# Offset columns from the partition number, one transfer for the hash matrix, and a replanned order: hashed attention and a feed-forward layer on one core

## The chip, the core and the metric

The kernel runs on one core of a Trainium2 chip. The metric is the device time of one execution in microseconds (us), lower is better. A core has TensorE (matrix products, PE in the profile; PEld are its weight loads), VectorE (DVE), ScalarE (ACT), GpSimd (POOL) and SyncE (SP, which here only issues transfers). Transfers are issued on a queue of SyncE or of ScalarE and are carried out by 16 DMA engines.

## What is computed

q, k and v have 4 batches of 8 heads, 768 positions and 64 columns; proj has 64 x 6 values. The feed-forward weights are 512 x 2048 and 2048 x 512. Every position of q and of k is hashed to a bucket by the signs of its six products with proj, and a query attends only to keys of its bucket:

```python
q_bits = (np.einsum('bhsd,dk->bhsk', q, proj) > 0).astype(np.int64)
k_bits = (np.einsum('bhsd,dk->bhsk', k, proj) > 0).astype(np.int64)
q_bucket = np.sum(q_bits * powers, axis=-1)
k_bucket = np.sum(k_bits * powers, axis=-1)
mask = q_bucket[:, :, :, None] == k_bucket[:, :, None, :]
scores = np.where(mask, scale * np.matmul(q, k.transpose(0, 1, 3, 2)), -1000000000.0)
attn = softmax(scores)             # with 1e-9 added to the sum
x = np.matmul(attn, v)             # heads side by side: 3072 x 512
out = gelu(x @ w_in) @ w_out
```

## The kernel before

**Staging.** A pass goes over a batch and some of its query positions; batch 0 is split in two passes (the first 256 queries, then 512), the other three are one pass each. Within a pass, a unit is 128 queries of one head: scores against all 768 keys (L987 in plain fp32 for batch 0, L989 and L990 in halves of 16 bits after it), their row maximum on VectorE (L993), exponential on ScalarE (L1007), a transposition, and the product with v. The feed-forward layer takes 256 queries at a time: 24 groups of hidden products (L1396), gelu, and output products (L1478).

**Hashing.** The bits are added to the operands of the score product as extra rows, so that a differing bit costs a large amount. For this each head's q and k are projected (`project`, L936 for batch 0, L695 later) with the matrix `hash32` or `hash16`, which hold proj and its negative side by side; ScalarE takes the sign with a small bias per partition (`sign`, L942, L701), and the signs are written as mask rows into the operands (`mask`, by `affine`, L460 and L464). The bias breaks ties: it is -TINY for some columns and +TINY for the others. It is an input of the program, `offset`, one value for each of 128 partitions.

**Set-up.** ScalarE's queue loads proj twice, into the upper and the lower 64 partitions of `praw` (L383, L384), and `offset` into `offs` (L386). VectorE writes the negative of proj beside it (L406) and copies both to `hash32` (L409). Two columns of bias are wanted, `off` and `off16`, since the two kinds of heads have their columns at different partitions. `set_up` makes them: GpSimd builds shift matrices from the identity (`copies`, L531), VectorE rounds `offs` to 16 bits (`narrow`, L538), TensorE moves it by two products (`spread`, L542), and VectorE copies the result to `both_offs` (`take`, L545). Each sign waits for this copy (`offs_ready`).

**What sets the order.** Nearly all work is a list of steps, each with an engine (or several to choose from), a cost in us, a key and the steps that it needs. `Plan.order` plays them through: whenever an engine is free, it takes the ready step with the lowest key, and some steps get their engine in this way too. `START` says when an engine begins. The keys come from the unit's number t and the numbers in `PAR`; the feed-forward products have keys from 1000 on. The outcome is a fixed order for each engine, in which instructions wait for their operands; a waiting instruction holds all behind it on its engine. SyncE's transfers stand in that order as well. Where TensorE has nothing ready, the plan may put in products of a blank tile (L419, up to 128 steps of four); nobody reads their result.

Of the kernel before, what the change touches and what calls it, by code (L numbers as in the profile page):

```python
# [38 lines left out]
    STICK=-82.49, LP_DVE=168.72, LP_Pool=131.55, KM=22.79, KM_ACT=-0.38, KM_DVE=21.62, KM_Pool=77.76, RN=-228.07,  # L39
    RT=-120.93, RC_ACT=-187.97, RC_DVE=104.4, XH_ACT=-169.94, XH_DVE=-58.71, XH_Pool=153.81, XL_DVE=2.29,  # L40
    XL_Pool=-84.29, VB=75.91, GU_DVE=376.97, GU_Pool=-283.34, SH_DVE=-141.74, SH_ACT=169, SH_Pool=-102.03,
    SF_DVE=106.59, SF_ACT=-91.62, SF_Pool=-105.46, SU=255.56, NM_DVE=139.91, NM_ACT=-81.24, NM_Pool=114.06,
    NM_SP=-82.67, NL_DVE=426.56, NL_Pool=109.97, NK_DVE=140.93, NK_ACT=118.24, NK_Pool=-152.1, Z=-98.92, VS0=-226.8,
    H0=1350.75, HL=-150.29, VS=-186.92, G2=45.62, HQ=-153.69, VQ=-322.44, in0=210.99, out0=-154.22, in1=106.47,
    out1=18.08, in2=-133.65, out2=-122.24, in3=462.36, out3=2.34, H1=390.62, H2=235.99, H3=74.68, H4=-91.19,
    H5=-484.96, H6=160.92, H7=182.63, MEV=-284.82, MGE=-95.53, MSP=-95.01, V0=-96.78, QK0=-173.32, QK1=188.62,
    QK2=101.09, MX0=117.31, MX1=-38.76, MX2=-22.52, EX0=-485.91, EX1=468.22, EX2=-110.13, NR0=17.49, NR1=108.73,
    NR2=80.71, HI0=-258.98, HI1=22.07, HI2=232.15, LO0=35, LO1=-160.32, LO2=2.65, PV0=-16.06, PV1=-698.65,
    PV2=-277.98, TR0=151.7, TR1=219.82, TR2=2.67, V1=-251.7, V2=66.98, Sin0=-94.82, Sin1=-40.21, Sin2=62.47,
    Sin3=-65.73, Sout0=12.07, Sout1=20.19, Sout2=-141.49, Sout3=15.82, Lin=572.06, Pin=97.32, Qin=138.76,  # L50
    Cin=-105.62, Min=-18.36, Lout=375.6, Pout=89.64, Qout=24.03, Cout=365.45, Mout=-620.71, G0=52.67, G1=-55.39,
    G3=17.42, G4=-204.1, G5=26.67, G6=177.05, G7=213.7, DUP0=-160.19, DUP1=-74.32, DUP2=842.69, LOW0=-36.13,
    LOW1=-187.95, LOW2=-265.14, PRJ0=293.66, PRJ1=118.05, PRJ2=248.42, MSK0=-16.31, MSK1=-34, MSK2=-4.17,
    DI_ACT=44.21, DI_DVE=54.03, DI_Pool=-87.05, WS_ACT=-12.67, WS_DVE=-97.95, WS_Pool=-164.14, WH_ACT=60.25,
    WH_DVE=76.08, WH_Pool=10.25, WL_ACT=-103.41, WL_DVE=147.58, WL_Pool=27.65, VH_ACT=90.01, VH_DVE=123.18,
    VH_Pool=-76.83, RND_ACT=-125.63, RND_DVE=144.01, RND_Pool=117.51, HI_ACT=-106.91, HI_DVE=738.91, HI_Pool=34.78,
    EV_ACT=28.16, EV_DVE=4.77, EV_Pool=-35.31, GH_ACT=-33.98, GH_DVE=180.18, GH_Pool=55.02, NS0=123.24, NS1=-168.39,
    NS2=409,
# [22 lines left out]
class Plan:  # L81
# [16 lines left out]
    START = {"PE": 1.1, "DVE": 4.2, "Pool": 1.3, "SP": 0.7, "ACT": 2.7}  # L98
# [176 lines left out]
def tile_bucket_attention_moe(  # L275
# [98 lines left out]
    def buf(step):  # L374
# [22 lines left out]
    offs16 = const.tile([P, 1], BF16, tag="offs16", name="offs16")  # L397
# [116 lines left out]
    def set_up():  # L514
# [22 lines left out]
        def narrow():  # L537
            nc.vector.tensor_copy(out=offs16, in_=offs)  # L538
# [1031 lines left out]
```

## Time and profile before

| | us |
|---|---|
| three timed runs | 884.11, 886.59, 887.58 (median 886.59) |
| span of the profiled execution, first to last instruction | 882.8 |
| TensorE busy | 861.6 |
| VectorE, ScalarE, GpSimd busy | 668.3, 626.8, 404.9 |

The span is that of one profiled execution; the timed runs have no profile, and their median lies 3.8 us above it. Busy time of TensorE counts the blank products too. Granted clock is the share of TensorE's 2.4 GHz that it was given in a stretch: 1.00, or 0.50 for 1.2 GHz. In the rows, "idle before" is the time for which an engine had nothing to run ahead of an instruction, and the name behind the arrow is what ended it.

### The profile page before, as it was taken

How to read it: one execution, taken by the hardware profiler on the slowest of the kernel's cores; microseconds unless marked ns; L12 is line 12 of the kernel's file. 1: busy time of each engine (PE TensorE's matmuls, PEld its weight loads, DVE VectorE, ACT ScalarE, POOL GpSimd, SP SyncE). 2: the span in 40 equal slices, each digit the busy share in tenths (PEclk: the TensorE clock that was granted, in tenths of full speed). 3: DMA queues.
4: the chain of work that ended last, by engine and by line, in shares of the span. 5: the costliest groups of instructions: out<-in, count | busy, mean ns of one | idle time of the engine just before them, and what ended most of it. 6: DMA issues, size and time to landing. Idle time of an engine off the chain costs nothing. (4 is left out here: it accounts for less than half of the span.)

```text
span 882.8 us, 17207 instructions
## 1 busy us (share of the span) xinstructions
PE 861.6 (98%) x6419; PEld 554.4 (63%) x6419; DVE 668.3 (76%) x1360; ACT 626.8 (71%) x1061; POOL 404.9 (46%) x524
## 2 busy tenths in 40 slices
PE   7999988999999999999999999999999999999998
PEld 4666565666747656657656656665666566676663
DVE  5888888898898998998887988889887883212122
ACT  3788767898888887988797977887886773222221
POOL 2367545676667656656373655454553230000000
PEclk6999999999999999999999999999999999999999
DMA  9652475116888697768675969586866593000000
GB/s 326 191 157 70 141 210 140 41 48 134 151 154 168 142 189 156 149 135 175 127 162 110 212 130 186 107 178 129 153 123 117 99 185 55 25 1 25 1 26 24
DMA packets 281955, 111.48 MB, mean 126 GB/s; under 512 B 228624, under 2 KB 269584, under 8 KB 281872
## 3 DMA queue, kind: packets, MB, share of 16 engines
q1 hardware_dynamic: 281568, 110.39, 57.3%
q8 instruction: 50, 0.82, 0.4%
q14 instruction: 33, 0.27, 0.1%
q10 hardware_dynamic: 304, 0.00, 0.0%
HBM read 42.73 MB, written 6.29 MB: 56 GB/s over the span
## 5 line engine op out<-in xcount | busy, mean ns | idle before, releaser
L1396 PE MATMUL hp<-x,Win 128*128 128x256 f16 x2304 | 268.0, 272 | 0.5 <-ACT h L1406 0.2
L1478 PE MATMUL hp<-Wout,g 128*128 128x512 f16 x1152 | 263.3, 379 | 0.0
L1396 PEld LDWEIGHTS <-Win 128*128 128x128 f16 x2304 | 223.7, 98 | 41.6 <-issue 5.4
L993 DVE TENSOR_REDUCE rows<-s 128x1 f32<-128x768 f32 x192 | 180.7, 949 | 17.5 <-PE s L987 8.4
L1478 PEld LDWEIGHTS <-g 128*128 128x128 f16 x1152 | 110.8, 98 | 124.6 <-issue 4.1
L1007 ACT ACTIVATE p<-s,rows 128x768 f32<-128x768 f32 x141 | 139.2, 988 | 19.6 <-POOL rows L464 12.7
L1406 ACT ACTIVATE h<-hp,ffs 128x512 f32<-128x512 f32 x96 | 65.4, 681 | 89.5 <-PE hp L1396 87.9
L989 PE MATMUL s<-Q 88*128 88x384 f16 x304 | 99.4, 327 | 3.9 <-ACT wraw L1007 2.0
L990 PE MATMUL s<-K 128*128 128x384 f16 x304 | 99.2, 326 | 0.0
L464 DVE TENSOR_SCALAR g<-h,ffs 128x512 f16<-128x512 f32 x29 | 15.3, 526 | 96.0 <-ACT h L1434 68.3
L1448 DVE SCALAR_TENSOR_TENSOR g<-h,ffs,g 128x512 f16<-128x512 f32 x96 | 77.8, 822 | 6.6 <-ACT g L460 4.2
L998 POOL TENSOR_SCALAR rows<-rows,hs 128x1 f32<-128x1 f32 x68 | 48.1, 708 | 75.0 <-DVE rows L993 60.9
L486 POOL TENSOR_TENSOR K<-raw,Q 64x768 f16<-64x768 f32 x41 | 73.5, 1793 | 3.4
L1161 PE MATMUL hp<-pt,vhl 128*64 128x512 f16 (+1 forms) x864 | 74.9, 327 | 0.2 <-ACT h L1406 0.2
L1025 DVE SCALAR_TENSOR_TENSOR hl<-p,rows,hl 128x768 f16<-128x768 f32 x60 | 62.7, 1046 | 3.8 <-ACT hl L460 3.8
L1161 PEld LDWEIGHTS <-vhl 128*64 128x64 f16 x864 | 47.8, 110 | 25.4 <-issue 7.3
L1007 ACT ACTIVATE wraw<-s,rows 128x768 f32<-128x768 f32 x51 | 50.3, 985 | 12.0 <-POOL rows L464 7.1
L464 POOL TENSOR_SCALAR Q<-sign 24x384 f16<-24x384 f16 (+1 forms) x59 | 38.4, 651 | 36.6 <-ACT sign L701 13.4
L464 POOL TENSOR_SCALAR rows<-rows 128x1 f32<-128x1 f32 x87 | 31.9, 367 | 45.9 <-ACT p L1007 32.8
L464 POOL TENSOR_SCALAR raw<-raw,hs 64x768 f32<-64x768 f32 x41 | 44.0, 1072 | 5.8 <-ACT Q L460 2.3
L1434 ACT ACTIVATE h<-h 128x2048 f32<-128x2048 f32 x24 | 45.9, 1911 | 0.4
L989 PEld LDWEIGHTS <-Q 88*128 88x128 f16 x304 | 29.7, 98 | 25.0 <-issue 6.9
(169 smaller groups left out, 1302.5 us busy)
## 6 DMA issues: line engine op xcount, KB each, us to landing
raw<-qk SPq DMA_DIRECT2D x26, 384.0 KB, 3.6
vraw<-v SPq DMA_DIRECT2D x24, 384.0 KB, 4.1
wraw<-w_in SPq DMA_DIRECT2D x16, 512.0 KB, 4.5
wraw<-w_out SPq DMA_DIRECT2D x16, 512.0 KB, 4.1
out<-o SPq DMA_DIRECT2D x11, 512.0 KB, 3.5
K<-Q SPq DMA_DIRECT2D x28, 96.0 KB, 2.8
Q<-qk SPq DMA_DIRECT2D x6, 384.0 KB, 8.2
Q<-Q SPq DMA_DIRECT2D x20, 96.0 KB, 2.7
```

The lines of the kernel that those rows point to most:

```text
L464: on.tensor_scalar(out=o, in0=x, scalar1=scale, scalar2=bias, op0=ALU.mult, op1=ALU.add)
L486: on.tensor_tensor(out=o, in0=x, in1=y, op=ALU.subtract)
L989: nc.tensor.matmul(to, aq[kk, qs], ak[kk, n], start=True, stop=False)
L990: nc.tensor.matmul(to, bq[:, qs], bk[:, n], start=False, stop=True)
L993: nc.vector.tensor_reduce(out=nm, in_=both(sp), axis=AX.XY, op=ALU.max, negate=True)
L1007: nc.scalar.activation(out=buf(ex).rearrange("p (b k) -> p b k", b=2), in_=both(sp), func=AF.Exp, scale=sc, bias=nb, accum_out=ssum,)
L1025: nc.vector.scalar_tensor_tensor(out=buf(hi)[:, 1], in0=buf(ex), scalar=r, in1=buf(hi)[:, 0], op0=ALU.mult, op1=ALU.subtract,)
L1161: nc.tensor.matmul(pv[j * D : (j + 1) * D], buf(vh)[:, tv, kt, j * D : (j + 1) * D], pt_all[:, slots(j), tp * KT + kt], start=kt == 0 and ...
L1396: nc.tensor.matmul(buf(pair[0])[:, j * ch[1] : (j + 1) * ch[1]], win_hl[:, f0 // WB1, tw, pr, f0 % WB1 : f0 % WB1 + P], x[:, tx, pr, : ch[1]],
L1406: nc.scalar.activation(out=values_of()[:, 2 * fp : 2 * fp + 2, :nt], in_=buf(pair[0])[:, : 2 * nt].rearrange("p (j k) -> p j k", j=2), fun ...
L1448: nc.vector.scalar_tensor_tensor(out=gt[:, 1, s2, :nt], in0=h[:, s2, :nt], scalar=sg, in1=gt[:, 0, s2, :nt], op0=ALU.mult, op1=ALU.subtract,)
L1478: nc.tensor.matmul(buf(banks[u]).rearrange("p (c f) -> p c f", c=NWB), gt[:, tg, f, u * P : (u + 1) * P], wout_hl[:, :, tw, ft], start=ft ...
```

## The change

- `offset` stays an input but is no longer loaded. A column of partition numbers (`place`) is made by an iota on GpSimd; VectorE masks it to 5 bits, compares it with 6, 12, 18 and 24, and adds the results up to `off` and `off16`: eight VectorE instructions outside the plan. The steps `copies`, the old `narrow`, `spread` and `take` go, and the sign no longer waits for them.
- proj is loaded by one transfer into all 128 partitions, with a source that names it twice.
- The two writes behind it (negative, and the copy to `hash32`) become a step of the plan on VectorE (`narrow`, key -1000); the projections of batch 0 (L936) and the largest value of proj need it.
- Planned costs are nearer to recorded durations, `START` of VectorE is 4.9 instead of 4.2 and of GpSimd 1.6 instead of 1.3, and all numbers in `PAR` are new, so that every engine's order is another one.

```diff
-    nc.scalar.dma_start(out=praw[:D, :NBIT], in_=proj)
-    nc.scalar.dma_start(out=praw[D:, :NBIT], in_=proj)
-    offs = const.tile([P, 1], F32, tag="offs", name="offs")
-    nc.scalar.dma_start(out=offs, in_=offset)
+    nc.scalar.dma_start(out=praw[:, :NBIT], in_=proj.unsqueeze(0).broadcast_to([2, D, NBIT]))
+    place = const.tile([P, 1], I32, tag="place", name="place")
+    nc.gpsimd.iota(place, pattern=[[0, 1]], base=0, channel_multiplier=1)
...
     nc.vector.tensor_scalar(
-        out=praw[:, NBIT:], in0=praw[:, :NBIT], scalar1=-1.0, scalar2=None, op0=ALU.mult
+        out=place, in0=place, scalar1=D // 2 - 1, scalar2=None, op0=ALU.bitwise_and
     )
-    nc.vector.tensor_copy(out=hash32[:, : 2 * NBIT], in_=praw)
+    for n, by in enumerate((2.0, 1.0, 2.0, 1.0)):
+        nc.vector.tensor_scalar(
+            out=over[:, n : n + 1], in0=place, scalar1=float((n + 1) * NBIT), scalar2=by * TINY,
+            op0=ALU.is_ge, op1=ALU.mult,
+        )
+    nc.vector.scalar_tensor_tensor(
+        out=off, in0=over[:, 0:1], scalar=-TINY, in1=over[:, 1:2], op0=ALU.add, op1=ALU.subtract
+    )
+    nc.vector.tensor_tensor(out=over[:, 4:5], in0=over[:, 2:3], in1=over[:, 3:4], op=ALU.subtract)
+    nc.vector.scalar_tensor_tensor(
+        out=off16, in0=off, scalar=over[:, 1:2], in1=over[:, 4:5], op0=ALU.subtract, op1=ALU.add
+    )
...
         def narrow():
-            nc.vector.tensor_copy(out=offs16, in_=offs)
-
-        def spread():
-            for n in range(2):
-                nc.tensor.matmul(buf(sp)[:, n : n + 1], shift[:, n], offs16, start=True, stop=True)
-
-        def take():
-            nc.vector.tensor_copy(out=both_offs, in_=buf(sp)[:, :2])
+            nc.vector.tensor_scalar(
+                out=praw[:, NBIT:], in0=praw[:, :NBIT], scalar1=-1.0, scalar2=None, op0=ALU.mult
+            )
+            nc.vector.tensor_copy(out=hash32[:, : 2 * NBIT], in_=praw)
...
-        c = add("Pool", 0.9, copies, -1000.0, [])
-        z = add("DVE", 0.07, narrow, -1000.0, [])
-        sp = add("PE", 0.2, spread, -1000.0, [c, z], takes="hp")
-        o = add("DVE", 0.07, take, -1000.0, [sp])
-        free(sp, [o])
-        m = add("DVE", 0.1, largest, key, [])
+        z = add("DVE", 0.25, narrow, -1000.0, [])
+        m = add("DVE", 0.1, largest, key, [z])
...
-        pp = add("PE", 0.75, project, key + PAR[f"PRJ{cl}"], [space], takes="hp", table="quarter", act=0.5)
-        sg = add("ACT", 0.1 + 0.833e-3 * HS + 0.186, sign, key + PAR[f"PRJ{cl}"], [pp, offs_ready])
+        pp = add("PE", 0.75, project, key + PAR[f"PRJ{cl}"], [space, hash_ready], takes="hp", table="quarter", act=0.5)
+        sg = add("ACT", 0.1 + 0.833e-3 * HS + 0.186, sign, key + PAR[f"PRJ{cl}"], [pp])
...
-                        "PE", (1.85 if bare else 1.32) * part, lambda j=j, hidden=hidden: hidden(j), LATE + n,
+                        "PE", (1.85 if bare else 1.31) * part, lambda j=j, hidden=hidden: hidden(j), LATE + n,
...
-                step = add("PE", (1.84 if bare else 1.31) * part * len(us) / (nt // P), output, LATE + n + PAR["G2"], needs)
+                step = add("PE", (1.84 if bare else 1.295) * part * len(us) / (nt // P), output, LATE + n + PAR["G2"], needs)
```

The keys that the prediction names are built from these numbers (scores t - QK, row maxima t - MX, remainders t + LO; the last digit is 1 for batch 0's second pass and 2 for the later batches): QK1 188.62 to 2137.85, QK2 101.09 to 1489.12, MX2 -22.52 to 3724.79, LO2 2.65 to -1446.53.

## Rows read from the trace of the kernel before

**Rows 1.** The page: busy time, share of the span and instructions of each engine.

```profile
PE 861.6 (98%) x6419; PEld 554.4 (63%) x6419; DVE 668.3 (76%) x1360; ACT 626.8 (71%) x1061; POOL 404.9 (46%) x524
```

**Rows 2.** Stretches of the span, TensorE alone: stretch, length, busy, clock, DMA.

```profile
0.00:13.00 13.00, 6.69 (x64) 0.79 0.81 278
13.00:24.60 11.60, 11.60 (x62) 0.50 1.05 386
30.00:160.00 130.00, 123.65 (x928) 1.00 0.47 135
160.00:740.00 580.00, 574.94 (x4396) 1.00 0.72 141
```

**Rows 3.** The same stretches, the blank products of L419 alone.

```profile
0.00:13.00 13.00, 5.75 (x52) 0.79 0.81 278
13.00:24.60 11.60, 3.95 (x38) 0.50 1.05 386
30.00:160.00 130.00, 8.29 (x116) 1.00 0.47 135
```

**Rows 4.** Timeline of VectorE, 0 to 13.5 us: start, length, instruction, idle before.

```profile
5.89 0.17 DVE L406 TENSOR_SCALAR praw<-praw 128x6 f32<-128x6 f32 x1 [4.93 <-DMA praw<-proj]
...
9.72 0.16 DVE L538 CAST offs<-offs 128x1 bf16<-128x1 f32 x1 [3.45 <-DMA offs<-offset]
```

**Rows 5.** Timeline of TensorE, 0 to 26 us.

```profile
6.32 0.85 PE L936 MATMUL hp<-Q,hash 64*32 64x384 f32 x8 [1.93 <-DVE hash L409]
...
12.93 2.90 PE L987 MATMUL s<-K,Q 76*128 76x384 f32 x4
15.76 1.51 PE L936 MATMUL hp<-Q,hash 64*32 64x384 f32 x8
...
24.68 0.85 PE L936 MATMUL hp<-Q,hash 64*32 64x384 f32 x8
```

**Rows 6.** Timeline of ScalarE, 0 to 13.5 us (ACTq: its queue issuing a transfer).

```profile
1.95 0.60 ACTq L386 DMA_DIRECT2D offs<-offset  x1
...
11.23 0.58 ACT L942 ACTIVATE sign<-hp,both_offs 128x384 f16<-128x384 f32 x1 [6.34 <-DVE both_offs L545]
```

**Rows 7.** Transfers by issue, short stretches before 3.3 us: size, us to landing.

```profile
praw<-proj ACTq DMA_DIRECT2D x1, 1.5 KB, 3.5
...
praw<-proj ACTq DMA_DIRECT2D x1, 1.5 KB, 4.5
offs<-offset ACTq DMA_DIRECT2D x1, 0.5 KB, 7.7
...
Q<-qk SPq DMA_DIRECT2D x1, 384.0 KB, 9.3
```

**Rows 8.** Timeline of SyncE, 0 to 12 us (issue of the second head).

```profile
2.75 0.51 SPq L921 DMA_DIRECT2D Q<-qk  x1
```

**Rows 9.** Timeline of GpSimd, 0 to 13 us.

```profile
1.83 0.65 POOL L531 TENSOR_SCALAR_AFFINE_SELECT shift<-shift 128x128 bf16<-128x128 bf16 x2
...
11.98 0.58 POOL L464 TENSOR_SCALAR Q<-sign 12x384 f32<-12x384 f16 x1 [8.48 <-DMA v_first<-v]
```

**Rows 10.** Packets: ScalarE's queue (q10) at 0 to 30, 3.2 to 3.75, 5.5 to 9.5 us.

```profile
q10 hardware_dynamic: 304, 0.00, 0.5%
...
q10 hardware_dynamic: 80, 0.00, 8.2%
...
DMA packets 650, 1.05 MB, mean 261 GB/s; under 512 B 177, under 2 KB 177, under 8 KB 650
q10 hardware_dynamic: 144, 0.00, 1.8%
```

**Rows 11.** Stretches, columns PE, PEld, DVE, ACT, POOL busy, clock, DMA, GB/s.

```profile
10.00:11.00 1.00, 0.61 (x7) 0.45 (x7) 0.97 (x3) 0.00 (x0) 0.00 (x0) 0.50 1.04 407
13.00:160.00 147.00, 140.65 (x1028) 89.97 (x1027) 128.85 (x278) 109.23 (x212) 79.77 (x124) 0.96 0.53 161
```

**Rows 12.** Waits of SyncE, 0 to 12 us: waited for, us, times, longest.

```profile
SPq L921 <- DMA offs<-offset: 2.4, 1, 2.4
```

More of the change, by code (lines that the diff above doesn't have):

```diff
@@ L54 @@
[L54 to L58, printed above, removed]
+    Cin=253.12, Cout=465.18, DI_ACT=-325.46, DI_DVE=2049.02, DI_Pool=1092.15, DUP0=-1000.93, DUP1=-642.95,
@@ L97 @@
     SAME = {"PE": 0.0, "DVE": 0.13}
-    START = {"PE": 1.1, "DVE": 4.2, "Pool": 1.3, "SP": 0.7, "ACT": 2.7}
+    START = {"PE": 1.1, "DVE": 4.9, "Pool": 1.6, "SP": 0.7, "ACT": 2.7}
     QUEUE = 2.0
@@ L506, in everywhere @@
         dg = add(affine_on("DI", P, True), 0, diagonal, key, [top], takes="diag", port=True)
-        pm = add("PE", 0.11, spread, key, [dg], takes="hp")
+        pm = add("PE", 0.06, spread, key, [dg], takes="hp")
         free(dg, [pm])
@@ L578, in set_up @@
         hi = add("DVE", 0.2, high, key, [sc])
-        return [add("DVE", 0.2, low, key, [hi])], o
+        return [add("DVE", 0.2, low, key, [hi])], z
     def head_scale(top, w, key, needs, n):
@@ L607, in back @@
             )
-        pm = add("PE", 0.06 + 0.08 * n, total, key, needs, takes="hp")
+        pm = add("PE", 0.06, total, key, needs, takes="hp")
         e = add("DVE", 0.07, exponent, key, [pm])
@@ L719, in head @@
                 on = {
-                    "DVE": (0.18, PAR["NK_DVE"]), "ACT": (0.53, PAR["NK_ACT"]), "Pool": (0.56, PAR["NK_Pool"])
+                    "DVE": (0.25, PAR["NK_DVE"]), "ACT": (0.53, PAR["NK_ACT"]), "Pool": (0.56, PAR["NK_Pool"])
                 }
@@ L942, in sign @@
             nc.scalar.activation(out=buf(space), in_=buf(pp)[:, :HS], func=AF.Sign, bias=off)
-        pp = add("PE", 0.75, project, key + PAR[f"PRJ{cl}"], [space], takes="hp", table="quarter", act=0.5)
-        sg = add("ACT", 0.1 + 0.833e-3 * HS + 0.186, sign, key + PAR[f"PRJ{cl}"], [pp, offs_ready])
+        pp = add("PE", 0.75, project, key + PAR[f"PRJ{cl}"], [space, hash_ready], takes="hp", table="quarter", act=0.5)
+        sg = add("ACT", 0.1 + 0.833e-3 * HS + 0.186, sign, key + PAR[f"PRJ{cl}"], [pp])
         free(pp, [sg])
@@ L1037, in unit @@
         plain = back is None
-        sp = add("PE", 1.3 if plain else 0.67, scores, t - PAR[f"QK{cl}"], made, takes="s", act=0.6 if plain else 0.84)
+        sp = add("PE", 1.3 if plain else 0.662, scores, t - PAR[f"QK{cl}"], made, takes="s", act=0.6 if plain else 0.84)
         mx = add("DVE", 0.87, top, t - PAR[f"MX{cl}"], [sp])
@@ L1083, in whole_turn @@
             step.append(
-                add("PE", 0.12 * (k1 - k0), lambda k0=k0, k1=k1, step=step: product(k0, k1, step), t + PAR[f"LO{cl}"], [ex, hold[0]], takes="hp")
+                add("PE", 0.11 * (k1 - k0), lambda k0=k0, k1=k1, step=step: product(k0, k1, step), t + PAR[f"LO{cl}"], [ex, hold[0]], takes="hp")
             )
@@ L1183, in weigh @@
                 )
-            xs = add("DVE", 0.08 + 0.27 * nt / TC, weigh, -10, [share, parts[-1], v_ready[b]])
+            xs = add("DVE", 0.08 + 0.34 * nt / TC, weigh, -10, [share, parts[-1], v_ready[b]])
         for n, ch in enumerate(chs):
@@ L1246, in tile_bucket_attention_moe @@
     used, owner = {}, {}
-    set16, offs_ready = set_up()
+    set16, hash_ready = set_up()
     v_ready = {}
@@ L1354, in second @@
             nc.vector.tensor_scalar(out=io, in0=inv2, scalar1=isg, scalar2=None, op0=ALU.mult)
-        a = add("DVE", 1.3, first, -10, [v_ready[b]] + [w_ready["in", c][0] for c in range(NSC)])
-        z = add("DVE", 0.3, second, -10, [a] + [w_ready["out", c][0] for c in range(NSC)])
+        a = add("DVE", 0.9, first, -10, [v_ready[b]] + [w_ready["in", c][0] for c in range(NSC)])
+        z = add("DVE", 0.17, second, -10, [a] + [w_ready["out", c][0] for c in range(NSC)])
         return a, z, ih, io, sg
```

46 lines of the change are left out of this document (21 added, 25 removed).

## Prediction

> **What bounds the kernel now.** I read the page's busy shares first. TensorE is busy for 861.6 of 882.8 us [rows 1], so an edit can only pay where TensorE idles, runs at its lower clock, or works on nothing. The stretches of the span tell where that is [rows 2]. From 160 to 740 us only 580.0 - 574.9 = 5.1 us are idle. Between 30 and 160 us it is 130.0 - 123.7 = 6.3 us, and in the first 13 us 6.3 us. Part of the busy time is padding: the matmuls of the blank tile (L419), whose result nobody reads, take 5.8 us before 13 us, 4.0 us between 13 and 24.6 us, and 8.3 us between 30 and 160 us [rows 3]. So the starved time is all of the first 13 us (but for one projection of 0.85 us), 4.0 us behind it, and 6.3 + 8.3 = 14.6 us in batch 0. Attention's first scores cannot be earlier than the first head's signs, and those I followed back on the timelines of VectorE, TensorE and ScalarE from 0 to 13 us.
>
> The reader sees there two waits in a row on VectorE. It idles 4.93 us until the projection matrix lands, writes praw and hash32 (L406, L409; the projection that waits for L409 starts at 6.32 us), then idles 3.45 us more at L538 until the offsets land, up to 9.72 us [rows 4, 5]. That projection was done at 7.17 us, and the first scores start at 12.93 us [rows 5]. ScalarE's first sign (L942) idled 6.34 us, and what ended that was both_offs, copied by L545; it starts at 11.23 us [rows 6]. Without that wait the sign could start when the projection ends, at about 7.4 us. The offsets are a transfer of 0.5 KB that needed 7.7 us from its issue at 1.95 us, where the two transfers of the projection matrix needed 3.5 and 4.5 us [rows 6, 7].
>
> **The change part by part.** *Offsets on chip.* Gone are one transfer, L538, the three affine selects L531, two matmuls and L545. The path to the first sign is then matrix, two VectorE writes, projection: 11.23 - 7.4 = 3.8 us earlier, if the matrix lands when it does now. VectorE goes on at 9.72 - 3.45 = 6.27 instead of 9.72 us [rows 4], and all that stood behind L538 moves up. These are one stall seen on two engines and count once: 3.8 us. What is late next is the second head. Its q, k transfer was issued at 2.75 us and landed 9.3 us later, at 12.05 us [rows 7, 8], and its projection ran at 15.76 us [rows 5]. Taken 3.8 us forward that is 12.0 us, so the gain just fits. The third head, projected at 24.68 us, stood behind most of the 4.0 us of blank matmuls [rows 3, 5], so it has room too.
>
> *What is added.* Eight VectorE instructions on one or a few columns. The nearest row is L538 with 0.16 us: 8 x 0.16 = 1.3 us [rows 4]. They need only the iota and fit into the 4.93 us in which VectorE now waits for the matrix [rows 4]: nothing on the path. If their order in the queue puts them behind that wait, they cost up to 1.3 us. An iota has no row. Pool's nearest one is 0.65 us for two of the selects L531 [rows 9], so I bound it by 0 and 0.65 us and take 0.3, as one select; Pool loses three selects and idles 8.48 us after its set-up [rows 9], so this is hidden either way. ScalarE issues two transfers less (0.60 us for that of the offsets [rows 6]); it idles 6.34 us before the sign, so nothing is gained.
>
> *Transfers.* While the offsets' packets were under way, the loads got 261 GB/s between 5.5 and 9.5 us [rows 10], against 407 GB/s between 10 and 11 us [rows 11]: (407 - 261) x 4 us = 0.58 MB, or 1.4 us of transfer for everything behind them. SyncE's issue of the third head also waited 2.4 us for the offsets [rows 12]. I add nothing for these, since the heads behind have room; they support the 3.8 us.
>
> *The matrix in one transfer.* The wait is not new: the projection already waited 1.93 us for L409 [rows 5]. But the two writes are now VectorE's first planned step, so everything VectorE has (decoding, maxima of v, row maxima) is queued behind the landing, and all other engines wait for VectorE. SyncE may wait for this transfer as it did for the offsets [rows 12]. One transfer of 128 rows is issued where the first of two is now, at about 0.7 us, while the second left at about 1.3 us. The bounds by rows: the first of the two now (64 rows) needs 3.5 us, so 4.2 us [rows 7]; the offsets (128 rows, one transfer, the same queue) needed 7.7 us, so 8.4 us. I take the middle, 6.3 us, so near today's 5.8 us that I leave the term at 0; the ends are worth 1.6 us less and 2.6 us more. The ends leave a gain of 5.4 or 1.2 us of the 3.8 us.
>
> The rows of the three transfers on ScalarE's queue make 304 packets, 64 + 64 + 128 rows and 3 x 16 more [rows 10], which I read as one closing packet from each of 16 DMA engines. The Trainium skill ("DMA: Bandwidth & Descriptors", section on how many engines a DMA uses, and the table behind it) says that the slowest dimension of the two access patterns sets how many engines share a transfer, and that a leading broadcast of c copies confines it to c engines. By that rule the new transfer, a broadcast of 2 copies of 64 rows, runs on two engines, 64 rows each; no run of the kernel before shows such a transfer. What it would cost is the second rival below.
>
> *Clock.* The granted clock fell to the lower level (1.2 GHz) in the gap and stayed at 0.50 from 13 to 24.6 us [rows 2]. The work other than blanks there was 11.6 - 4.0 = 7.6 us, so at the full clock 3.8 us less. With the gap shorter the clock may hold, or not, since TensorE still waits for the matrix first; I take 0 and keep 0 to 3.8 us for the range.
>
> *The new order.* The keys in PAR are all new, the recorded durations change TensorE's planned costs by a few per cent (1.32 to 1.31 a hidden product, 1.31 to 1.295 an output product). Scores now rank far ahead in passes 1 and later (t - 2137, t - 1489 against t - 189, t - 101), row maxima (t - 3725) and score remainders of batch 1 on (t - 1447) ahead of VectorE's feed-forward steps (-9, -10). The feed-forward work stays at 1000 and fills the rest, and the matmuls are the same. So the sum of TensorE's work is fixed, and the order moves only the starved time: at best 14.6 us of batch 0 and 5.1 us behind it. From the other side no row bounds it; were the idle share of the steady stretch to double, 5.1 us more. The trace can't tell the sign; with planned costs nearer to the recorded ones I take 1 us of gain.
>
> *The end* is not touched: last product at 878.9 us, drain, store.
>
> Sum: 3.8 + 0 + 0 + 1.0 = 4.8 us off the profiled 882.8 us, 878.0 us. The median of the timed runs lies 886.6 - 882.8 = 3.8 us over the span, so 881.8 us; I say 882.
>
> **The rivals.** *The order is worth more.* A good part of the 14.6 us starved in batch 0 goes, or the clock holds. For it: most of this is padding and waits of under 1.5 us that other work could fill. Against it: VectorE is 128.9 of 147 us busy there [rows 11], so it can't be much denser. Half of the 14.6 us beside the 3.8 us gives 886.6 - 11.1 = 875.5 us.
>
> *The matrix comes late (slower).* If the single transfer goes through few DMA engines, its rows queue one behind another. On 16 engines the matrix's rows moved at 5 packets per engine in 0.55 us, 0.11 us each, and the offsets' at 9 per engine in 4 us, 0.44 us each [rows 10]. With 64 rows on each of two engines, 60 more than today's 4, the landing comes 60 x 0.11 = 6.6 or 60 x 0.44 = 26.4 us behind 4.2 us: at 10.8 or 30.6 us. It decides from a landing at 9.6 us on: the first sign would start 7.4 - 5.8 = 1.6 us behind it, so then it is as late as now. At 0.11 us the loss is 1.2 us, at 0.44 us 21.0 us; at 0.22 us, between them by ratio, the landing is at 17.4 us and the loss 7.8 us, so 894 us. For it: the offsets show that a small transfer can hold up for 7.7 us, and VectorE and SyncE both queue behind this one. Against it: 128 rows of 24 bytes are little, and at the pace of the nearest row (the matrix itself) the loss is hardly seen. This is the page's rule made into a time.
>
> *The head's gain is used up later.* The early loads move at 386 GB/s on average from 13 to 24.6 us [rows 2], so the transfers could set the pace of the first heads whatever VectorE does; or the new order starves TensorE by some 4 us more in the steady stretch. Then nothing is left: 886.6 us. Against it: the room of the second and third head above.
>
> **How the numbers follow.** The forecast has 0.48, the better order 0.15, the late matrix 0.25, the used-up gain 0.12. About 0.5% (4.4 us) is what a measurement of this kernel can tell from no change. The forecast lies 4.6 us below the median, so it is halved: 0.24 faster, 0.24 same. The better order is faster, 0.15. The late matrix is same at the low pace, 0.07, else slower, 0.18. The used-up gain is same 0.09, slower 0.03. Faster 0.39, same 0.40, slower 0.21. Range: the forecast alone, with the ends of its landing and 4 us of order, is 876 to 888; down to 874 takes in most of the better order, up to 894 the late matrix at the middle pace.
>
> **What would show it.** Right: in the profile after, the first sign starts near 7.5 us, ending VectorE's only long wait at about 6 us; no wait for an offset; first scores near 9 us; the second head's projection near 12 us. The eight small instructions lie before the matrix's landing. Wrong: the praw transfer's time to landing above 9 us, with fewer packets beyond its rows than 16, and VectorE's first planned step behind it. The order is judged by idle and blank time between 30 and 160 us (14.6 us now) and idle between 160 and 740 us (5.1 us). The prediction falls if the matrix lands after 9.6 us, or if the starved time behind 30 us changes by more than 5 us.

## The result and the profile after

The changed kernel takes 874.3 us (median of five runs, 873.32 to 878.38) where the kernel before takes 884.75 us beside it. The ratio is 0.9886, with an interval of 0.9861 to 0.9911: 10.4 us less, where 4.8 us were forecast. A second set of nine runs, taken later beside its own runs of before, has a median of 875.77 us and a ratio of 0.9925 [0.9901, 0.9949], so 8.2 us less. The profiled execution is the slowest of the first five, 878.38 us; its span is 876.6 us, 1.8 us less than its time, and so it stands in every run that has both. The page after, against [rows 1]:

```profile
span 876.6 us, 17169 instructions
...
PE 859.8 (98%) x6385; PEld 548.2 (63%) x6385; DVE 673.3 (77%) x1357; ACT 629.1 (72%) x1072; POOL 413.8 (47%) x527
```

The stretches of the span after, TensorE alone (columns as in [rows 2]), and below the "..." the blank products in two of them, which answer to [rows 3]:

```profile
0.00:13.00 13.00, 10.36 (x82) 1.00 0.89 316
13.00:24.60 11.60, 9.64 (x85) 0.96 1.05 385
30.00:160.00 130.00, 124.58 (x898) 0.98 0.44 130
160.00:740.00 580.00, 576.54 (x4416) 1.00 0.71 140
...
0.00:13.00 13.00, 6.58 (x60) 1.00 0.89 316
30.00:160.00 130.00, 5.10 (x72) 0.98 0.44 130
```

In batch 0 (30 to 160 us) TensorE idles 5.4 us and works on blanks for 5.1: 10.5 us starved where it was 14.6. In the steady stretch it idles 3.5 us (0.4 more on blanks) where it was 5.1. VectorE, ScalarE and TensorE up to the first scores after (timelines as in [rows 4 to 6]):

```profile
6.13 0.17 DVE L539 TENSOR_SCALAR praw<-praw 128x6 f32<-128x6 f32 x1 [5.17 <-DMA praw<-proj]
...
7.67 0.69 DVE L755 SCALAR_TENSOR_TENSOR Win<-wraw,Win 128x512 int32<-128x512 int32 x1
8.28 0.15 DVE L405 TENSOR_SCALAR place<-place 128x1 int32<-128x1 int32 x1
...
8.85 0.15 DVE L413 SCALAR_TENSOR_TENSOR both_offs<-over 128x1 f32<-128x1 f32 x1
...
9.09 0.58 ACT L935 ACTIVATE sign<-hp,both_offs 128x384 f16<-128x384 f32 x1 [4.21 <-DVE both_offs L413]
...
6.57 1.50 PE L929 MATMUL hp<-Q,hash 64*32 64x384 f32 x8 [1.14 <-DVE tops L545]
...
10.71 1.53 PE L980 MATMUL s<-K,Q 76*128 76x384 f32 x4
```

The matrix lands at about 6.1 us, near the 6.3 us taken. But ScalarE's sign still idles 4.21 us, and what ends it is still `both_offs`: the eight instructions that write the offsets stand at 8.28 to 9.4 us in VectorE's queue, behind the wait for the matrix and the first decoding of a weight (L745 to L755), though the iota that they need is done at 0.95 us. The first sign came forward from 11.23 to 9.09 us only, where about 7.5 us was expected, and the first scores stand at 10.71 us, not near 9 us. Yet the first scores took 1.53 us where they took 2.90 [rows 5].

**A balance for all kernels.** The span is working time of TensorE (busy without blanks) plus starved time (idle and blanks). The busy time comes from the page, the blanks from the groups of instructions by line; here that of before and of after (last three numbers ahead of the releasers: busy, mean ns, idle before):

```profile
L419 PE MATMUL hp<-blank 128*128 128x128 bf16 x224 | 19.6, 254 | 3.0 <-DVE hash L402 1.0 <-DVE both_offs L545 0.6 <-ACT sign L701 0.6
```

```profile
L429 PE MATMUL hp<-blank 128*128 128x128 bf16 x192 | 15.9, 245 | 3.3 <-DVE pt L474 1.7 <-DVE hash L401 1.0 <-DVE hs L583 0.4
```

Before: 861.6 - 19.6 = 842.0 us of work and 882.8 - 842.0 = 40.8 us starved. After: 843.9 and 32.7 us. The real products are the same in number, save two, so working time differs by the speed at which they ran. The two numbers are not independent, since products that run slowly fill gaps: after (twice), e3 and e7 share the order and the place of the offsets, and they have 32.3 to 35.3 us starved, the most in e7, which worked the least. Differences of up to 3 us of starved time between single executions say little. All kernels of this study:

| kernel | median us | ratio to before [95%] | span | working | starved |
|---|---|---|---|---|---|
| before | 884.75 | | 882.8 | 842.0 | 40.8 |
| after, first profile | 874.3 | 0.9886 [0.9861, 0.9911] | 876.6 | 843.9 | 32.7 |
| after, second profile | 875.77 | 0.9925 [0.9901, 0.9949] | 873.2 | 840.9 | 32.3 |
| e1 offsets on chip, order of before | 878.88 | 0.9940 [0.992, 0.996] | 878.3 | 843.5 | 34.8 |
| e2 whole new head, order of before | 876.78 | 0.9930 [0.991, 0.995] | 874.4 | 838.9 | 35.5 |
| e11 as e2, offsets first | 875.38 | 0.9899 [0.9875, 0.9923] | 873.5 | 840.3 | 33.2 |
| e3 after, two transfers | 877.36 | 0.9924 [0.9909, 0.9939] | 876.0 | 841.4 | 34.6 |
| e4 after, wait for offsets back | 878.65 | 0.9941 [0.9927, 0.9955] | 876.8 | 841.3 | 35.5 |
| e5 after, offsets first | 873.05 | 0.9891 [0.9864, 0.9919] | 871.3 | 838.1 | 33.2 |
| e6 after, no blanks | 876.35 | 0.9928 [0.9902, 0.9954] | 874.6 | 848.2 | 26.4 |
| e7 after, ten more blanks | 877.24 | 0.9942 [0.9909, 0.9975] | 873.9 | 838.6 | 35.3 |
| e8 as e5, matrix on two queues | 875.28 | 0.9901 [0.9872, 0.9929] | 874.7 | 841.5 | 33.2 |
| e9 as e5, no blanks | 876.62 | 0.9919 [0.9887, 0.9951] | 875.0 | 848.9 | 26.1 |
| e10 as e8, second head's load first | 877.18 | 0.9918 [0.9892, 0.9944] | 876.1 | 841.4 | 34.7 |

The experiments ran in three sets, each on one chip beside its own runs of before (e1 to e4: 884.21 us; the repetition of after, e5 to e7: 883.99; e8 to e11: 885.57). Within a set medians may be compared; across sets the ratios. Working and starved time are of one profiled execution each.

### The profile page after: what moved, and what is told of

The parts are those of the page before. It is cut to its first block, busy times and chain, and to the rows that moved or that the text cites. A ratio compares the mean times of both kernels' runs of the same rounds, so it can differ in the third digit from the quotient of the medians.

```text
span 876.6 us, 17169 instructions
## 1 busy us (share of the span) xinstructions
PE 859.8 (98%) x6385; PEld 548.2 (63%) x6385; DVE 673.3 (77%) x1357; ACT 629.1 (72%) x1072; POOL 413.8 (47%) x527
## 4 chain that ended last, share of the span: by engine, by line
PE 80%; DVE 7%; ACT 6%; DMA 3%; issue 2%; POOL 2%; ACTq 0%; DVEq 0%; POOLq 0%
PE hp L1471 27%; PE hp L1389 25%; PE hp L1154 8%; PE s L982 5%; PE s L983 5%; PE s L980 4%; DVE rows L986 2%; PE hp L1145 2%; PE hp L1062 2%; ACT p L1000 1%; PE hp L688 1%; ACT Q L470 1%; DVE Win L750 1%; ACT wraw L1000 1%; DMA praw<-proj 1%
## 5 line engine op out<-in xcount | busy, mean ns | idle before, releaser
L1000 ACT ACTIVATE p<-s,rows 128x768 f32<-128x768 f32 x141 | 139.2, 988 | 26.1 <-POOL rows L474 9.4
L496 POOL TENSOR_TENSOR K<-raw,Q 64x768 f16<-64x768 f32 x45 | 80.5, 1789 | 3.8
L1018 DVE SCALAR_TENSOR_TENSOR hl<-p,rows,hl 128x768 f16<-128x768 f32 x66 | 73.2, 1112 | 7.9 <-POOL hl L474 6.2
L474 DVE TENSOR_SCALAR g<-h,ffs 128x512 f16<-128x512 f32 x27 | 14.5, 538 | 83.2 <-ACT h L1427 58.6
L1441 DVE SCALAR_TENSOR_TENSOR g<-h,ffs,g 128x512 f16<-128x512 f32 x96 | 74.9, 797 | 2.4 <-POOL g L474 0.6
L991 POOL TENSOR_SCALAR rows<-rows,hs 128x1 f32<-128x1 f32 x61 | 36.9, 605 | 69.4 <-DVE rows L986 67.7
L474 POOL TENSOR_SCALAR rows<-rows 128x1 f32<-128x1 f32 x98 | 39.3, 401 | 48.2 <-ACT p L1000 20.8
L474 POOL TENSOR_SCALAR raw<-raw,hs 64x768 f32<-64x768 f32 x45 | 47.1, 1047 | 8.0 <-ACT Q L470 3.7
L980 PE MATMUL s<-K,Q 76*128 76x384 f32 x112 | 44.4, 525 | 1.4 <-ACT p L1000 1.1
L474 POOL TENSOR_SCALAR hl<-p,rows 128x768 f16<-128x768 f32 x32 | 32.2, 1007 | 27.8 <-DMA pt<-hl 13.4
```

Of the source, the lines that this page charges most:

```text
L474: on.tensor_scalar(out=o, in0=x, scalar1=scale, scalar2=bias, op0=ALU.mult, op1=ALU.add)
L496: on.tensor_tensor(out=o, in0=x, in1=y, op=ALU.subtract)
L980: nc.tensor.matmul(to, q[:, qs], k[:, n], start=True, stop=True)
L1000: nc.scalar.activation(out=buf(ex).rearrange("p (b k) -> p b k", b=2), in_=both(sp), func=AF.Exp, scale=sc, bias=nb, accum_out=ssum,)
L1018: nc.vector.scalar_tensor_tensor(out=buf(hi)[:, 1], in0=buf(ex), scalar=r, in1=buf(hi)[:, 0], op0=ALU.mult, op1=ALU.subtract,)
L1441: nc.vector.scalar_tensor_tensor(out=gt[:, 1, s2, :nt], in0=h[:, s2, :nt], scalar=sg, in1=gt[:, 0, s2, :nt], op0=ALU.mult, op1=ALU.subtract,)
```

## The experiments

**e1: the offsets alone.** The order of before is kept for every engine, only the offsets are made on chip; both transfers of the matrix stay.

```diff
-    offs = const.tile([P, 1], F32, tag="offs", name="offs")
-    nc.scalar.dma_start(out=offs, in_=offset)
+    place = const.tile([P, 1], I32, tag="place", name="place")
+    nc.gpsimd.iota(place, pattern=[[0, 1]], base=0, channel_multiplier=1)
```

> The kernel before, its order unchanged on every engine, with the offset columns made on chip: no offset transfer, no shift matrices, no L538, L542, L545. The matrix still comes in two transfers. Theory 'head': the stall at L538 was on the path, so the first sign moves from 11.2 us to 8 to 9 us (the eight small VectorE instructions may lie behind the landing, as in the changed kernel), the first scores from 12.9 to about 10.7 us, and the time falls by 2 to 4 us from 884.8, to 881 to 883 us. Theory 'order': the old order was planned for other times and gives the gain back behind the first heads; the first scores come early but the time stays within 1 us of 884.8.

Measured: 5.3 us less than before in its set (878.88 against 884.21), from 875.65 to 881.64. The first sign stands at 9.27 us and the first scores at 10.48, behind the decoding here too. So the removed wait, with the transfer that it stood for, is worth more than the 3.8 us of its path, although that path came forward by 2.0 us only.

**e2: the whole new head.** As e1, with the single transfer and the two writes as a step of the plan.

```diff
-    nc.scalar.dma_start(out=praw[:D, :NBIT], in_=proj)
-    nc.scalar.dma_start(out=praw[D:, :NBIT], in_=proj)
+    nc.scalar.dma_start(out=praw[:, :NBIT], in_=proj.unsqueeze(0).broadcast_to([2, D, NBIT]))
```

> As the run before it, and with the matrix in one transfer and its two writes inside the plan's first VectorE step: the changed kernel's whole head under the old order. Theory 'head': like the run before it within 1 us, 881 to 883 us, since the single transfer lands at about 6 us, where the second of two landed at 5.8 us; the rest of the 10.4 us that the change gained (6 to 8 us) is then the new order's. If the head carries all of the gain, 874 to 876 us. Theory 'order': within 1 us of 884.8.

Measured: 7.4 us less than before. As TensorE's order is that of before, its timeline can be laid beside [rows 5] instruction by instruction:

```profile
10.31 1.58 PE L992 MATMUL s<-K,Q 76*128 76x384 f32 x4
11.82 0.85 PE L941 MATMUL hp<-Q,hash 64*32 64x384 f32 x8
...
14.45 2.17 PE L428 MATMUL hp<-blank 128*128 128x128 bf16 x36
16.55 0.85 PE L941 MATMUL hp<-Q,hash 64*32 64x384 f32 x8
```

and e1's, with the same instructions again:

```profile
10.48 2.90 PE L994 MATMUL s<-K,Q 76*128 76x384 f32 x4
13.31 1.50 PE L943 MATMUL hp<-Q,hash 64*32 64x384 f32 x8
...
18.33 2.74 PE L433 MATMUL hp<-blank 128*128 128x128 bf16 x36
21.00 0.85 PE L943 MATMUL hp<-Q,hash 64*32 64x384 f32 x8
```

Against before, e2's first scores start 2.6 us earlier (12.93 to 10.31), its third head's projection 8.1 us (24.68 to 16.55), its span ends 8.4 us earlier. So 5.5 us are gained between the first scores and the third head, where not a single instruction differs: before needs 11.75 us for them, with TensorE at the lower of its levels (1.2 GHz), e2 6.24 us at 2.4 GHz. e1 starts its scores 0.17 us later than e2, but stays at the lower speed up to 21 us; it is 4.5 us late at the third head and 3.9 us in the span. The runs of e2 say the same: four with a mean granted clock of 0.996 or more took 875.99 to 876.88 us, the two with 0.992 took 879.59 and 880.42. The fastest of e1 (mean 1.00) took 875.65. So in the profiles e1 and e2 differ by the speed that they got; why one got it and the other not isn't shown. Their medians are 2.1 us apart, but the intervals of their ratios overlap widely, and the single transfer itself is not seen.

**e3: the changed kernel with two transfers.**

```diff
-    nc.scalar.dma_start(out=praw[:, :NBIT], in_=proj.unsqueeze(0).broadcast_to([2, D, NBIT]))
+    nc.scalar.dma_start(out=praw[:D, :NBIT], in_=proj)
+    nc.scalar.dma_start(out=praw[D:, :NBIT], in_=proj)
```

> The changed kernel, its order unchanged, with the matrix in two transfers of 64 rows again. The changed kernel's ScalarE queue shows 130 packets, 128 rows and 2 more, so its single transfer ran on two engines. Theory 'two engines cost nothing here': two transfers land at 5 to 6 us as well, and the time stays within 1.5 us of 874.3. Theory 'two engines cost': with 16 engines each the matrix lands at 4.5 to 5 us, and the time is 1 to 1.5 us lower than that of the changed kernel, 873 us.

Measured: a ratio of 0.9924, against 0.9925 for the repetition of the changed kernel. VectorE's write behind the landing starts at 5.88 us (after: 6.13 us). By the times one transfer costs and gives nothing here (e3 has about 2 us more starved time, in one execution). What it is made of shows in the packets on ScalarE's queue in the first 30 us (after, the transfers view), where [rows 10] had 304:

```profile
q10 hardware_dynamic: 130, 0.00, 0.2%
```

That is 128 rows and 2 more, where the three transfers of before had 16 more each. By the reading of the prediction (one closing packet from each engine) the transfer runs on two engines. The Trainium skill ("DMA: Bandwidth & Descriptors", Rules for kernel authors) says that a leading broadcast of c copies confines a transfer to at most c engines; the 2 packets beyond the rows agree with that. But all 130 pass between 3.2 and 6.2 us, 65 for each engine, at most 0.05 us each, beside loads at 363 GB/s. The price per row that the late-matrix rival took from the rows of before (0.11 to 0.44 us) was at least two times too high.

**e4: the wait for the offsets put back.** The changed kernel, with the offset transfer and a copy behind it in VectorE's first step; nothing uses the copy.

```diff
+    nc.scalar.dma_start(out=offs, in_=offset)
...
             nc.vector.tensor_copy(out=hash32[:, : 2 * NBIT], in_=praw)
+            nc.vector.tensor_copy(out=offs16, in_=offs)
```

> The changed kernel, its order unchanged, with the offset transfer put back behind the matrix on ScalarE's queue, and one VectorE copy that waits for it in the plan's first step; nothing uses the copy. Theory 'head': the transfer lands at 8.5 to 10 us, VectorE and all behind it go 2 to 4 us later, first scores at 13 to 14 us, and the time rises by 2 to 4 us, to 876 to 878 us. Theory 'order': the new order has slack behind the first heads that takes this up; the time stays within 1 us of 874.3.

Measured: 878.65 us; by the ratios 1.4 us slower than the repetition of the changed kernel, and within its set 1.3 us slower than e3. VectorE's wait, and the packets with their rates from 5.5 to 9.5 us:

```profile
8.90 0.16 DVE L546 CAST offs<-offs 128x1 bf16<-128x1 f32 x1 [2.69 <-DMA offs<-offset]
...
DMA packets 731, 1.23 MB, mean 308 GB/s; under 512 B 173, under 2 KB 173, under 8 KB 731
```

Its first sign, its first scores, and below the "..." TensorE behind 30 us with the blank products last:

```profile
11.64 0.58 ACT L939 ACTIVATE sign<-hp,both_offs 128x384 f16<-128x384 f32 x1 [6.75 <-DVE both_offs L416]
...
13.27 2.88 PE L984 MATMUL s<-K,Q 76*128 76x384 f32 x4
...
30.00:160.00 130.00, 124.57 (x910) 1.00 0.45 134
160.00:740.00 580.00, 576.03 (x4411) 1.00 0.71 140
...
30.00:160.00 130.00, 5.10 (x72) 1.00 0.45 134
```

The packets from 5.5 to 9.5 us in the second profile of after:

```profile
DMA packets 686, 1.44 MB, mean 359 GB/s; under 512 B 47, under 2 KB 47, under 8 KB 686
```

The loads are slower beside the offsets, by (359 - 308) x 4 us = 0.2 MB, about 0.6 us of transfer and not 1.4; the first profile of after has 389 GB/s there, which would make it 0.8 us. And the wait of 2.69 us costs less than under the old order: the new order, with the wait in it, is already 5.6 us faster than before. None of this comes from an earlier start: e4's first sign stands at 11.64 us and its first scores at 13.27, each a little later than before (11.23 and 12.93). It is the order's, and behind 30 us TensorE starves less: 5.4 + 5.1 us in batch 0 and 4.0 us idle in the steady stretch, 14.5 us where 14.6 + 5.1 = 19.7 us were. Wait and order draw on the same starved time.

**The repetition of the changed kernel**, unchanged, as a base for the next three.

> The changed kernel once more, beside the runs of this call. Both theories: 873.5 to 875 us, with runs at a mean granted clock of 1.00 at the lower end and runs at 0.994 up to 878 us.

Measured: 875.77 us. Its span is 3.4 us below that of the first profile, with the same starved time (32.3 against 32.7 us). Its first scores run at the lower speed, 2.88 us, up to 19.0 us; the first profile ran its first scores at full speed and fell to 0.50 from 23.8 to 34.0 us. Where the lower speed falls differs between executions of one and the same program. What it costs differs too: both executions have a mean granted clock of 0.994, but 840.9 and 843.9 us of work.

**e5: the offsets first.** The eight instructions move from the set-up into VectorE's first step of the plan, ahead of the write that waits for the matrix; nothing else changes.

```diff
         def narrow():
+            nc.vector.tensor_scalar(
+                out=place, in0=place, scalar1=D // 2 - 1, scalar2=None, op0=ALU.bitwise_and
+            )
...
             nc.vector.tensor_scalar(
                 out=praw[:, NBIT:], in0=praw[:, :NBIT], scalar1=-1.0, scalar2=None, op0=ALU.mult
             )
```

> The changed kernel with the eight offset instructions moved ahead of the two writes in the plan's first VectorE step, so that they run before the matrix lands instead of behind the first decoding; nothing else changes. Theory 'path': the first sign comes when the projection ends, 8.1 us instead of 9.1 us, and decoding gets 1.0 us of VectorE back, so the time falls by 1 us to about 873.5 us. Theory 'clock': the time goes by whether the granted clock holds in the first 35 us; an earlier sign changes nothing that is seen beyond it, and the time stays within 0.5 us of the changed kernel's, with the same spread.

Measured: 873.05 us, all six runs between 872.82 and 873.83, each with a mean granted clock of 1.00; 2.7 us below the changed kernel in the same set. The timelines of VectorE, ScalarE and TensorE:

```profile
2.06 0.22 DVE L536 SCALAR_TENSOR_TENSOR both_offs<-both_offs,over 128x1 f32<-128x1 f32 x1
5.66 0.17 DVE L539 TENSOR_SCALAR praw<-praw 128x6 f32<-128x6 f32 x1 [3.38 <-DMA praw<-proj]
...
7.01 0.58 ACT L935 ACTIVATE sign<-hp,both_offs 128x384 f16<-128x384 f32 x1 [2.22 <-PE hp L929]
...
6.10 0.85 PE L929 MATMUL hp<-Q,hash 64*32 64x384 f32 x8 [0.67 <-DVE tops L545]
...
9.23 1.53 PE L980 MATMUL s<-K,Q 76*128 76x384 f32 x4 [0.29 <-DVE K L459]
```

Now the offsets are done at 2.3 us inside the wait, and the sign waits for the projection alone, at 7.01 us. This is the head that the prediction described. It has the lowest median of the study, and in its set all six runs lie below all nine of the changed kernel; by the ratios (0.9891) it is no faster than the first five runs of the changed kernel (0.9886). Of its gain over the second profile of after, 1.9 us in the span, the starved time has no part (33.2 against 32.3); working time is 2.8 us less, and its first heads run at full speed, where the second profile of after has the lower one up to 19 us.

**e6 and e9: no blanks.** The 192 blank products are left out, from the changed kernel (e6) and from e5 (e9).

```diff
-            for k in range(4):
-                nc.tensor.matmul(buf(step)[:, :P], blank, blank, start=True, stop=True)
+            pass
```

> The changed kernel with all its 192 blank products left out, the rest of the order as it is. Theory 'clock': the granted clock stays at 0.50 for longer in the first 30 us, and the first heads' products cost up to twice as much there; with 4 to 6 us of them the time rises by 3 to 5 us, to 877 to 879 us. Theory 'starved': blank products stand in the way of real ones now and then (4 us ahead of the third head's projection in the kernel before), so without them the time falls by up to 2 us, to 872 us.

> The run e5 with all blank products left out. All six runs of e5 had a mean granted clock of 1.00, those of the changed kernel mostly 0.994. Theory 'clock': the clock that holds from 6.1 us on is what e5 gains over the changed kernel beside 1 us of path; without blanks it is at 0.50 up to about 20 us as in the changed kernel without blanks, and the time rises by 2 to 4 us, to 875 to 877 us. Theory 'path': blank products are worth nothing, as in the changed kernel (876.4 without, 875.8 with); the time stays within 0.5 us of 873.0.

Measured: e6 0.6 us slower than the changed kernel in its set, no difference; e9 876.62 us, by the ratios 2.5 us slower than e5 and by the medians of two sets 3.6; the fastest run of e9 (875.26) is slower than the slowest of e5 (873.83), though on another chip. e9's TensorE, and the granted clock of the stretch:

```profile
6.07 1.50 PE L928 MATMUL hp<-Q,hash 64*32 64x384 f32 x8 [6.07 <-DVE tops L544]
...
9.27 2.90 PE L979 MATMUL s<-K,Q 76*128 76x384 f32 x4 [1.57 <-DVE K L458]
...
22.78 2.45 PE L979 MATMUL s<-K,Q 76*128 76x384 f32 x4
25.16 0.85 PE L928 MATMUL hp<-Q,hash 64*32 64x384 f32 x8
...
8.00:24.00 16.00, 14.73 (x45) 1.00 1.05 388
```

Its first scores start at the same moment as in e5, but every product takes nearly twice its time up to about 24 us. So the blanks are worth something in e5, where the speed holds with them and not without them, and nothing that the times show in the changed kernel. Why isn't shown. In its second profile TensorE idles 1.67 us behind the first projection and its scores are slow, in e5 0.59 and 0.29 us and they are fast; but e7, next, idles 1.18 and 0.39 us there with fast scores.

**e7: a fuller first gap.** The changed kernel with 50 instead of 40 blank products ahead of the first projection.

```diff
-            for k in range(4):
+            for k in range(5 if n < 10 else 4):
```

> The changed kernel with ten more blank products ahead of the first projection, so that TensorE has work from 1.0 to about 6.5 us, when the matrix is there, instead of to 5.4 us. Theory 'clock': the first projection runs at the full clock (0.85 us instead of 1.50 us) or the clock holds more often behind it; the runs lie closer together at 873 to 874 us. Theory 'path': the extra products end at about the time at which the projection can start, and the time stays within 0.5 us of the changed kernel's.

Measured: 877.24 us, from 875.01 to 885.22. In its profile the projection runs at full speed (6.42 us, 0.86) and the scores too. Here are the first scores of the second profile of after, which are slow, and then those of e7:

```profile
10.32 2.88 PE L980 MATMUL s<-K,Q 76*128 76x384 f32 x4
```

```profile
10.26 1.53 PE L980 MATMUL s<-K,Q 76*128 76x384 f32 x4 [0.39 <-DVE K L474]
```

Yet the spans of the two are nearly the same, 873.2 and 873.9 us: e7 works 2.3 us less and starves 3.0 us more. And e7's runs scatter over 10 us, with mean clocks from 0.988 to 1.00. So filling the gap ahead of the first projection doesn't hold the speed in every execution, and what decides it stays open.

**e8 and e10: the matrix sooner.** e5 with the halves of the matrix on the queues of ScalarE and SyncE (e8), and then the second head's load ahead of the weights (e10).

```diff
-    nc.scalar.dma_start(out=praw[:, :NBIT], in_=proj.unsqueeze(0).broadcast_to([2, D, NBIT]))
+    nc.scalar.dma_start(out=praw[:D, :NBIT], in_=proj)
+    nc.sync.dma_start(out=praw[D:, :NBIT], in_=proj)
```

```diff
+    loads = [k for k, s in enumerate(steps) if s.engine == "SP"]
+    steps.insert(loads[1], steps.pop(loads[4]))
```

> The run e5 (offset instructions first) with the matrix in two halves of 64 rows, the upper on ScalarE's queue and the lower as SyncE's first transfer, so that neither stands behind loads of weights. Theory 'matrix': everything hangs on the matrix until 5.7 us; it now lands at 4.2 to 4.6 us, the first sign moves from 7.0 to about 5.9 us, and the time falls by 1 us, to 872 us. Theory 'loads': what is late next is the second and third head, whose transfers land at 9.8 and 15.5 us whatever the matrix does; the first scores come earlier, but the time stays within 0.5 us of 873.0.

> The run e8 with SyncE's transfer of the second head moved ahead of the three transfers of w_in. Theory 'loads': the second head lands at 6 to 7 instead of 9.8 us and its projection can follow the first scores at once, while decoding starts 1 us later; with the matrix early the time falls by 1 to 2 us, to 871 to 872 us. Theory 'VectorE': VectorE is the engine that is short in the first 100 us, and with decoding later it gains nothing: 873 us or up to 1 us more.

Measured: 875.28 and 877.18 us, neither better than e5. The matrix is there at 3.2 us and the first sign at 6.21 us (e8), but the first scores start only at 10.23 us. VectorE's longest wait in the first 30 us, e8 and e10:

```profile
DVE Win L746 <- DMA wraw<-w_in: 3.2, 1, 3.2
```

```profile
DVE Win L746 <- DMA wraw<-w_in: 4.6, 1, 4.6
```

VectorE stands at the first decoding of a weight, whose load is now later than the matrix, and the mask rows that the scores need are queued behind it. A second head's load ahead of the weights makes this wait longer (4.6 us), and brings nothing; the 1.9 us between the medians of e10 and e8 lie within the scatter of their runs. What is late next behind the offsets and the matrix is therefore VectorE's own queue, with a weight's load at its head.

**e11: e5's head under the order of before.** e2 with the eight instructions first, as in e5.

> The run e2 (new head under the old order) with the offset instructions first, as in e5; against e5 it leaves the order alone, with the same head and, if the clock holds here too, the same clock. Theory 'order counts a little': starved time of TensorE between 30 and 160 us stays at 13.8 us here against 10.2 us in e5, so 875 to 876.5 us, 2 to 3.5 us above e5. Theory 'head is all': the order's gain is given back elsewhere and the time is within 1 us of e5's 873.0.

Measured: 875.38 us, ratio 0.9899, where e5 with the new order has 0.9891: 0.7 us by the ratios, 2.3 by the medians of two sets. Starved time is 33.2 us in both. With e2 to e5 it completes a table of starved time (idle and blanks) by head and order, and, from the stretches, by place:

| | order of before | order of after |
|---|---|---|
| wait for the offsets | 40.8 (before) | 35.5 (e4) |
| offsets behind the matrix | 35.5 (e2) | 32.3, 32.7 (after), 35.3 (e7) |
| offsets first | 33.2 (e11) | 33.2 (e5) |

The stretches from 0 to 30 and 30 to 160 us, all of TensorE and then blanks alone, of e11:

```profile
0.00:30.00 30.00, 26.21 (x218) 1.00 0.98 344
30.00:160.00 130.00, 124.36 (x943) 0.99 0.47 134
...
0.00:30.00 30.00, 8.66 (x100) 1.00 0.98 344
30.00:160.00 130.00, 8.29 (x116) 0.99 0.47 134
```

and of e5:

```profile
0.00:30.00 30.00, 24.93 (x232) 1.00 0.98 344
30.00:160.00 130.00, 123.59 (x908) 1.00 0.44 130
...
0.00:30.00 30.00, 10.36 (x132) 1.00 0.98 344
30.00:160.00 130.00, 3.79 (x52) 1.00 0.44 130
```

The new order starves TensorE for 10.2 us in batch 0 instead of 13.9, but for 15.4 us in the first 30 us instead of 12.5. With the best head it only moves the starved time forward, as far as one execution of each tells. Behind the wait it gains 5.3 us of it. With the offsets behind the matrix after has 3 us less than e2; but e7, which ran its first heads at full speed as e2 did, has no less.

## Why the prediction was right in its direction and too small in its size

**The offsets path: right cause, wrong way.** The wait at L538 was on the path, and removing it is worth 5.3 us alone (e1), where 3.8 us were taken. The step that failed is "nothing on the path" for the eight instructions. The prediction named the other case, the queue that puts them behind the wait, at up to 1.3 us. It is what happened, and it costs 1.7 to 2.1 us of the first sign (8.68 and 9.09 us in the two profiles of after against 7.01 us in e5), since they came to stand behind the decoding too; in the set of e5 2.7 us of time go with it. They are no steps of the plan, and came to stand in the queue behind steps that could not run yet. That isn't so of every such instruction: in e1 the two writes of the matrix are no steps either, and run ahead of the decoding.

**The clock: a mis-sized term.** It was taken as 0 with 3.8 us as the other end. Under the same order it gave 5.5 us between the first scores and the third head where the speed held (e2), of which 1.8 us are the blanks in between (2.17 us where 3.95 stood, [rows 3]); that leaves 3.7 us of work, almost the whole of the other end. Where it didn't hold, 3.9 us of span were missing (e1 against e2). For the changed kernel itself its share isn't shown. In the first profiles it even counts against the change (working time 842.0 and 843.9 us), as that execution is the slowest; the median run of after, with a mean clock of 1.00, lies 4 us below it, but has no profile. In the second profile of after working time is 1.1 us less than before.

**The order: right sign, too small, and not a term of its own.** One microsecond was forecast. Behind the wait it is worth 5.6 us (e4 against before), with the offsets behind the matrix 0.4 or 3.9 us by the ratios of e2 and of the two sets of the changed kernel, with the offsets first 0.7 us by the ratios and no starved time. The prediction said that it falls if the starved time behind 30 us changes by more than 5 us, judged in batch 0 and the steady stretch. Of the 19.7 us there, 10.5 + 3.5 = 14.0 us are left in the first profile of after and 14.7 us in the second, 5.7 and 5.0 us less; so by its own sign its small price for the order failed in the first and stands on the edge in the second. e4, with no earlier head, has 5.2 us less there. Starved time as a whole fell by 8.1 and 8.5 us, where head and order were to bring 4.8. The sum of the prediction added head and order; they share one reserve: alone they give 7.4 us (e2) and 5.6 us (e4), together 8.2 and 10.4 us. What the keys, the planned costs and `START` each do in it wasn't tried apart. Whether the order also shortens the work stays open: e5 has 2.2 us less of it than e11, but e11 was for a short time at the lower speed in batch 0 (0.99 in its stretch).

**The single transfer: right.** It landed at about 6.1 us (6.3 taken), on two engines. The late-matrix rival rested on a price per row that these runs don't show; it decides from a landing at 9.6 us on, which was not reached in any profile.

**What is late next: wrong.** The second head's transfer was named, but TensorE does not wait for it: its projection runs at 12.17 us, straight behind the first scores. That this is the "near 12 us" of the prediction is luck, as it was to come from the transfer, with first scores near 9 us. VectorE's queue is next (e8, e10).

**The offset between span and time: too large.** Taken as 3.8 us by setting one profiled span against the median of other runs; runs that have both show 1.8 us. The profile of before belonged to a run of about 884.6 us, not of 886.6, and with 1.8 us the same sum gives 879.8 us: 2.0 of the 7.7 us between the forecast of 882 us and the measured 874.3 us come from this.

**The range.** 874.3 us lies 0.3 us above its lower end, which was set to take in most of the better order. That the first set lies inside is as much luck as foresight; the gain was more than twice the forecast one.

**The rivals.** "The order is worth more" gave 875.5 us and was the closest in time; half of the 14.6 us in batch 0 did not go (4.1 and 3.3 us went), and the clock held for the first scores in one profile of after and not in the other. It was right that the order is worth more by itself (e4), and wrong to add that to the whole of the head. "The gain is used up later" fell: the times stay lower, and e2's 8.1 us at the third head are 8.4 us at the end.

## What to carry to other kernels

Split TensorE's span into working and starved time for each kernel: the first tells of its speed, the second of the order, though slow products hide starved time; and two edits that fill the same starved time don't add up, so try each without the other. Where a kernel starts with a wait, price the work that follows at both speeds, since first scores that came 2.6 us earlier ended the span 8.4 us earlier in e2, and 2.5 us earlier only 4.5 in e1. An instruction that is ready early gains nothing if the queue has it behind a waiting one: look at where it stands, and make it a step of the plan.

## What the runs showed of the hardware

The row of the granted clock doesn't always tell the speed: e1 (up to 21 us) and e9 (up to about 24 us) have 1.00 while scores take 2.90 us instead of 1.53; before had the same 2.90 us at a recorded 0.50. The length of a known product is the safer sign. The Trainium skill ("TensorE: Matmul & The Clock Gate", Seeing it yourself) warns that the clock's events in a trace have been seen to be unreliable; the rows of e1 and e9 agree. The speed in the first 35 us differs between executions of one program. In e2 the two runs with the lower mean clock are the slower ones, by 3.5 us; in the second set of after the mean doesn't tell them apart (0.994 at 875.04 and at 879.04 us). Only e5 has a recorded mean of 1.00 in all its runs, and they lie within 1.0 us. A transfer of 128 rows of 24 bytes on two engines was as quick as two of 64 rows on sixteen (5.6 and 6.1 us to VectorE's write in the two profiles of after, 5.9 us in e3), while beside one of 128 rows of 4 bytes (e4) the loads got 308 GB/s where after had 359 and 389. An iota over 128 partitions took 0.13 us on GpSimd, where 0.3 was estimated.
